# Score chunks copied out by ScalarE and folded in bf16 by VectorE, and merge transposes done by DMA, in an attention block with its gradients

## The chip, the cores and the metric

The kernel runs on one core of a Trainium2 chip. The core has five engines that run side by side, each with its own instruction queue worked off in order: TensorE (PE in the profile; PEld is its weight load), VectorE (DVE), ScalarE (ACT), GpSimd (POOL) and SyncE (SP), which here issues nearly all DMA transfers. Waits between engines go by semaphores. Data lies in SBUF (128 partitions); TensorE writes to PSUM, which VectorE and ScalarE read and GpSimd doesn't use here. The metric is the device time of one execution in microseconds; lower is better.

## The reference

A branchformer layer, forward and all gradients, for x and grad_out of shape [2, 4000, 144] in bf16. Cut to what matters:

```python
xa = layernorm(x)
q, k, v = split(xa @ w_qkv)
p = softmax(q @ k.T * 144 ** -0.5)             # 4000 x 4000 for each of the 2 batches
glob = (p @ v) @ w_att_out
u, g = split(gelu(xa @ w_mlp_in))
loc = (u * conv5(layernorm(g), dw_csgu)) @ w_mlp_out
m = concat(glob, loc)
out = x + (m + conv5(m, dw_merge)) @ w_merge
# and the vjp of out for grad_out: gradients of x and of the seven weights
```

`conv5` is a depthwise convolution with five taps along the sequence.

## The kernel before

A batch of 4000 positions is cut into 32 tiles of 125; both batches make 64 tiles, numbered through. A batch's position p * 32 + j lies on partition p in tile j, so that a shift along the sequence becomes a shift of the tile's number.

**The attention loop** (`phase_att`). Step s of its loop makes the scores of tile s and finishes earlier tiles. A tile's 4000 scores come in four chunks of 1000 (`c2` = 0 to 3). `products(q)` calls `quad`, which issues eight matmuls: scores of tile s, chunk q (two of 500 columns), and for tile s - 1, chunk q ^ 1, the product dP of the output gradient with the values (two of 500); each first over 128 rows of the contraction (L1304), then over the 16 left over (L1311). The results lie in two PSUM buffers `ps`, of which the pool `ps_sg` has exactly two.

- The scores' buffer is emptied by `S_min`: VectorE writes the negated scores in bf16 into `Pbuf` and their least into a column of `nm` in the same pass (L1326). After the fourth chunk a reduction over four columns gives the tile's least (L1328).
- `P_exp` turns a chunk of `Pbuf` into exponentials in place, on ScalarE, with that least as bias (L1332). All four chunks need the whole tile's least.
- dP's buffer is emptied by `PdP`: ScalarE copies it to `Sbuf` in bf16 (L1342), and VectorE multiplies it with `Pbuf` (L1344).
- `P_tr` (L1336) and `st_half` (L1518) transpose `Pbuf` and `Sbuf` into `PT` and `ST` by DMA, in halves of 16 blocks, for the products over keys: `Y_half` (L1353, with a reciprocal and small operations on three engines behind it) and `Z_half` (L1391).
- `X_group` (L1438) accumulates, over two tiles at a time, the gradient of the normalised input; VectorE adds it to `acc` in SBUF (L1444).

**The local branch** (`local_units`, L571 to L710) is cut into small units that are strewn over the attention loop's steps, for tiles 2 to 26 with batch 0 and again for tiles 34 to 60 with batch 1. Between the two, batch 1 is prepared (`prep_late`).

**The merge** (`Merge`, `tr_pieces`, `out_g`). After the attention, the forward output needs the transposes of attention output (h = 0) and local product (h = 1), 36 blocks each with the halo, for each batch: `transposes` does up to eight blocks with TensorE into one PSUM buffer (L1642), and ScalarE copies them to `YT[h]` (L1643), which for h = 0 is the storage of `goT` of batch 1. The 16 columns left over go the same way to `YS` (L1647, L1648). `out_g` multiplies from `YT` and `YS` (L1809, L1811). Both batches use the same `YT`, batch 0 first. Meanwhile `fill` issues matmuls for a weight gradient (`Hps`, L1724).

**The order.** A class `Planner` takes all instructions of the kernel and gives each engine a fixed order, by a list schedule with its own costs. Ready instructions are taken by their place in the program plus a lead from the table `LEAD`, whose keys name the stage (H, A, B, E, T), the engine, the tile and the size, and for some tiles the number of the instruction within a step.

Of the kernel before, what the change touches and what calls it, by code (L numbers as in the profile page):

```python
# [744 lines left out]
class Planner:  # L745
# [488 lines left out]
def phase_att(k, W, SS, A, head, E0, E1, prep, hooks):  # L1234
# [21 lines left out]
    PT = ab.tile([128, NB, 128], BF, name="PT")  # L1256
    ST = ab.tile([128, NB, 128], BF, name="ST")
    QBs = ab.tile([PB, NPB, 2, D], BF, name="QBs")
    qbr = [ab.tile([128, 512], BF, name="qb%d" % i) for i in range(3)]
    znr = [ab.tile([128, 256], BF, name="zn%d" % i) for i in range(2)]  # L1260

    def clr():
# [60 lines left out]
    def S_min(i, c2, src):  # L1323
        if c2 == 0:
            NM[i] = small.tile([PB, 5], F32, tag="nm", name="nm")
# [944 lines left out]
```

## Time and profile before

| | us |
|---|---|
| median of 3 runs | 1250.8 (1249.42 to 1252.87) |
| profiled execution | 1250.75 |
| its span, first to last instruction | 1249.0 |
| PE busy | 1182.0 (95%), 14424 matmuls |
| DVE busy | 1113.2 (89%), 3209 instructions |
| ACT busy | 867.3 (69%), 1590 |
| POOL busy | 348.1 (28%), 520 |

Granted TensorE clock: 0.998 of full speed. How to read the profile's lines: a group of instructions is given by line, engine, operation, names out<-in and shapes, then the count, the busy time in us and the mean ns of one, then the idle time of the engine just before them and what ended it. A row of a window has start:end, its length, then for each engine its busy time and the number of instructions, then the granted clock, the share of the DMA engines and GB/s. In a row of the timeline the two numbers in front are start and duration in us. In a row of one tile or line, three durations in ns are the least, the median and the largest. An operation's duration includes a part in which the next one has already begun, so in a full engine the distance of two starts is shorter. PE's busy time includes modelled ends; a busy PE is not PE at its peak.

### The profile page before, as it was taken

The numbers are of one execution on the slowest core, as the hardware profiler recorded it, in microseconds if no ns is written. First come the engines' busy times: TensorE is split into PE (matmuls) and PEld (weight loads), VectorE is DVE, ScalarE is ACT, GpSimd is POOL, SyncE is SP. The second block draws the span as 40 slices with busy tenths as digits, with TensorE's granted clock in tenths as the row PEclk, the third lists the DMA queues.
The fourth block names the chain that finished last, engine by engine and source line by source line (L and its number), as shares of the span: only waits on it lengthen the run. The fifth ranks groups of instructions, "written<-read, shape, count | busy, mean of one in ns | idle before, by whom it ended". The sixth has DMA issues, their size and how long they took to land.

```text
span 1249.0 us, 36648 instructions
## 1 busy us (share of the span) xinstructions
PE 1182.0 (95%) x14424; PEld 954.4 (76%) x14424; DVE 1113.2 (89%) x3209; ACT 867.3 (69%) x1590; POOL 348.1 (28%) x520
## 2 busy tenths in 40 slices
PE   6999999999999988999999999999999989999998
PEld 4677777777777767787777777777777767799997
DVE  8579999999999998987799999999999997779515
ACT  5897776777777666677877777777777756654741
POOL 7131323223232313301232332323232231033400
PEclk9999999999999999999999999999999999999999
DMA  4777787788787769998897877787968769967522
GB/s 137 148 151 152 138 181 141 159 170 153 161 160 143 157 132 189 177 162 190 170 170 140 167 154 151 162 162 144 183 138 168 149 132 197 208 173 182 148 56 57
DMA packets 662847, 193.94 MB, mean 155 GB/s; under 512 B 637619, under 2 KB 657093, under 8 KB 662653
## 3 DMA queue, kind: packets, MB, share of 16 engines
q1 hardware_dynamic: 661544, 190.20, 75.6%
q8 instruction: 113, 1.85, 0.6%
q0 software_dynamic: 592, 1.18, 0.3%
q14 instruction: 60, 0.49, 0.1%
q10 hardware_dynamic: 538, 0.21, 0.1%
HBM read 23.14 MB, written 16.69 MB: 32 GB/s over the span
## 4 chain that ended last, share of the span: by engine, by line
DVE 46%; PE 31%; ACT 10%; DMA 6%; issue 5%; POOL 1%; SPq 1%; DVEq 0%; ACTq 0%; POOLq 0%
DVE Pbuf L1326 12%; PE X L1438 7%; DVE Sbuf L1344 7%; DVE acc L1444 6%; PE ps L1304 5%; PE yz L1391 4%; DVE l_prod L637 3%; ACT Pbuf L1332 3%; PE yz L1353 3%; PE ps L1311 2%; PE po L1809 2%; ACT Sbuf L1342 2%; PE Hps L1724 2%; DMA PT<-Pbuf 2%; DMA ST<-Sbuf 1%
## 5 line engine op out<-in xcount | busy, mean ns | idle before, releaser
L1342 ACT CAST Sbuf<-ps 125x1000 bf16<-125x1000 f32 x252 | 251.8, 999 | 135.0 <-PE ps L1311 132.4
L1326 DVE TENSOR_SCALAR_CACHE_REDUCE Pbuf<-ps 125x1000 bf16<-125x1000 f32 x256 | 305.8, 1195 | 29.5 <-PE ps L1311 29.0
L1332 ACT ACTIVATE Pbuf<-Pbuf,nm 125x1000 bf16<-125x1000 bf16 x256 | 286.2, 1142 | 41.1 <-DVE nm L1328 41.1
L1438 PE MATMUL X<-QBs,Sbuf 125*125 125x144 bf16 x2048 | 296.4, 229 | 10.2 <-DVE acc L1444 5.5
L1438 PE MATMUL X<-QBs,Pbuf 125*125 125x144 bf16 x2048 | 291.7, 226 | 1.4 <-POOL QBs L1375 1.4
L1438 PEld LDWEIGHTS <-Sbuf 125*125 125x125 bf16 x2048 | 259.7, 137 | 30.4 <-issue 28.7
L1304 PE MATMUL ps<-xaT_m,qt 128*125 128x500 bf16 x1024 | 262.4, 375 | 14.7 <-DVE Pbuf L1326 8.7
L1438 PEld LDWEIGHTS <-Pbuf 125*125 125x125 bf16 x2048 | 260.7, 137 | 12.4 <-issue 12.0
L1444 DVE TENSOR_TENSOR acc<-X,acc 125x432 f32<-125x432 f32 (+1 forms) x373 | 200.1, 549 | 10.7 <-PE X L1438 9.2
L1344 DVE TENSOR_TENSOR Sbuf<-Sbuf,Pbuf 125x1024 bf16<-125x1024 bf16 x252 | 183.2, 729 | 3.2 <-ACT Sbuf L1342 2.5
L1304 PEld LDWEIGHTS <-qt 128*125 128x125 bf16 x1024 | 124.6, 137 | 60.2 <-issue 17.0
L1391 PE MATMUL yz<-xa_aug,ST 125*125 125x144 bf16 x2048 | 150.3, 228 | 12.4 <-ACT ty L1369 9.3
L1391 PEld LDWEIGHTS <-ST 125*125 125x125 bf16 x2048 | 140.1, 138 | 20.8 <-issue 14.8
L1353 PE MATMUL yz<-xa_aug,PT 125*125 125x145 bf16 x2048 | 148.6, 228 | 3.7 <-DMA PT<-Pbuf 2.6
L1353 PEld LDWEIGHTS <-PT 125*125 125x125 bf16 x2048 | 137.5, 137 | 14.0 <-issue 9.2
L1375 POOL TENSOR_TENSOR QBs<-g,g 125x144 bf16<-125x144 f32 x64 | 33.8, 528 | 285.7 <-ACT g L1374 271.9
L1311 PEld LDWEIGHTS <-qt 16*125 16x125 bf16 x1024 | 36.2, 128 | 98.9 <-issue 98.9
L1311 PE MATMUL ps<-XR,qt 16*125 16x500 bf16 x1016 | 110.9, 420 | 0.0
L637 DVE TENSOR_TENSOR l_prod<-ring,Wc 125x720 bf16<-125x720 bf16 x128 | 70.8, 576 | 0.0
L574 POOL TENSOR_SCALAR l_a<-l_sq 125x576 bf16<-125x576 bf16 x32 | 23.8, 743 | 165.7 <-ACT l_sq L572 157.4
L682 POOL TENSOR_TENSOR A_dwc<-l_fl,A_dwc 128x512 f32<-128x512 f32 (+2 forms) x48 | 39.8, 829 | 62.0 <-ACT l_fl L681 61.3
L665 POOL TENSOR_SCALAR l_w<-ring,nc,c 125x144 f32<-125x144 bf16 x60 | 34.8, 585 | 77.6 <-DVE nc L661 28.7
(545 smaller groups left out, 2067.4 us busy)
## 6 DMA issues: line engine op xcount, KB each, us to landing
Yn_d<-yn SPq DMA_DIRECT2D x64, 35.2 KB
Zn_d<-zn SPq DMA_DIRECT2D x64, 35.2 KB
ug_d<-ugr SPq DMA_DIRECT2D x32, 70.3 KB
PT<-Pbuf SPq DMA_TRANSPOSE x126
ST<-Sbuf SPq DMA_TRANSPOSE x126
go_h<-in_grad_out_dram SPq DMA_DIRECT2D x8, 252.0 KB
Yg<-Yn_d SPq DMA_DIRECT2D x8, 252.0 KB
Yg<-ug_d SPq DMA_DIRECT2D x8, 252.0 KB
```

Of the source, the lines that this page charges most:

```text
L637: nc.vector.tensor_tensor(prod[:, bi].rearrange("p a b -> p (a b)"), ring[:, a, p + bi:p + bi + 5, :].rearrange("p a b -> p (a b)"), W.Wc[ ...
L682: nc.gpsimd.tensor_tensor(acc, fl[r0:r1, 0:n], acc, op=ALU.add)
L1304: mm = nc.tensor.matmul(pp[r // 2][:, r % 2, 0:CH], QT[i][:, 2 * h, 0:PB], bs(i)[0].xaT_m[:, c * CH:(c + 1) * CH], start=True, stop=False)
L1311: nc.tensor.matmul(pp[r // 2][:, r % 2, 0:CH], QT[i][rs, 2 * h + 1, 0:PB], xr, start=False, stop=True)
L1326: nc.vector.tensor_scalar(pv(Pbuf, i % NPB, c2), src, -1.0, 3.0e38, op0=ALU.mult, op1=ALU.min, accum_out=NM[i][:, c2:c2 + 1])
L1332: nc.scalar.activation(v, v, ACT.Exp, bias=NM[i][:, 4:5], scale=-1.0)
L1342: nc.scalar.copy(pv(Sbuf, i % NDB, c2), src)
L1344: nc.vector.tensor_tensor(sc, sc, pchunk(i % NPB, c2), op=ALU.mult)
L1353: nc.tensor.matmul(Y, PT[0:PB, j, 0:PB], S.xa_aug[:, j, 0:D + 1], start=(j == 0), stop=(j == NB - 1))
L1391: nc.tensor.matmul(Z, ST[0:PB, j, 0:PB], S.xa_aug[:, j, 0:D], start=(j == 0), stop=(j == NB - 1))
L1438: nc.tensor.matmul(X[:, jj, :], l, r, start=(n_ == 0), stop=(n_ == len(ops) - 1))
L1444: nc.vector.tensor_tensor(av, X[:, 0:nj, :], av, op=ALU.add)
```

## The change

1. In `S_min`, chunks 0 and 2 (`SA`) no longer take VectorE's combined pass. ScalarE copies them from PSUM to `Pbuf`, negated. Once chunk 2 is there, VectorE takes the element-wise minimum of both chunks into a new tile `fold` (1000 wide), folds that onto itself twice (500, 250), and reduces the 250 left into the column of `nm` of chunk 2. Chunks 1 and 3 stay as they were. The last reduction now covers columns 1 to 3.
2. In the merge, batch 1's blocks for `YT` go through `turn`: GpSimd copies four blocks into one of three new tiles `ym` (partitions 125 to 127 of which stay zero), and a DMA transpose on SP's queue writes them to `YT`. That is 18 copies and 18 transposes. Batch 0 still uses TensorE. For this `YT` has blocks of 128 columns instead of 125, so `goT` of both batches grows by 108 columns.
3. The table `LEAD` is replaced by another, longer one: some 530 entries where there were some 170. It is cut out below.

```diff
     LEAD = {
-        "H ACT raw 144": -41, "H SP go_q 576": 145, "H DVE lnst 6": -4,
...
+        "H SP x_tp 1152": -167, "H DVE mhalf 32": -38, "H DVE wz 256": -50,
...
     }
...
     QBs = ab.tile([PB, NPB, 2, D], BF, name="QBs")
+    SA = (0, 2)
+    fold = ab.tile([PB, 2 * CH], BF, name="fold")
...
     def S_min(i, c2, src):
+        pb = i % NPB
         if c2 == 0:
             NM[i] = small.tile([PB, 5], F32, tag="nm", name="nm")
-        nc.vector.tensor_scalar(pv(Pbuf, i % NPB, c2), src, -1.0, 3.0e38, op0=ALU.mult, op1=ALU.min, accum_out=NM[i][:, c2:c2 + 1])
+        if c2 in SA:
+            nc.scalar.activation(pv(Pbuf, pb, c2), src, ACT.Copy, scale=-1.0)
+            if c2 == SA[-1]:
+                f = fold[:].rearrange("p (h a b) -> p h a b", h=2, b=PB)
+                nc.vector.tensor_tensor(f, pv(Pbuf, pb, SA[0]), pv(Pbuf, pb, SA[1]), op=ALU.min)
+                for w in (500, 250):
+                    nc.vector.tensor_tensor(fold[:, 0:w], fold[:, 0:w], fold[:, w:2 * w], op=ALU.min)
+                nc.vector.tensor_reduce(NM[i][:, c2:c2 + 1], fold[:, 0:250], axis=AX.X, op=ALU.min)
+        else:
+            nc.vector.tensor_scalar(pv(Pbuf, pb, c2), src, -1.0, 3.0e38, op0=ALU.mult, op1=ALU.min, accum_out=NM[i][:, c2:c2 + 1])
         if c2 == 3:
-            nc.vector.tensor_reduce(NM[i][:, 4:5], NM[i][:, 0:4], axis=AX.X, op=ALU.min)
+            nc.vector.tensor_reduce(NM[i][:, 4:5], NM[i][:, 1:4], axis=AX.X, op=ALU.min)
...
-        engs[0](dstm[:, j0 * PB:(j0 + n) * PB].rearrange("p (a b) -> p a b", b=PB), pm[:, 0:n, 0:PB])
+        engs[0](dstm[:, j0:j0 + n, 0:PB], pm[:, 0:n, 0:PB])
...
-        self.YT = [S1.goT, pm_.tile([128, NH * PB], BF, name="YT1")]
+        self.YT = [t[:].rearrange("p (a b) -> p a b", b=128) for t in (S1.goT, pm_.tile([128, NH * 128], BF, name="YT1"))]
+        self.ym, self.nym = [pm_.tile([128, 4, 128], BF, name="ym%d" % i) for i in range(3)], 0
+        for t in self.ym:
+            k.nc.gpsimd.memset(t[96:128], 0.0)
...
+    def turn(self, b, h, j0, n):
+        nc = self.k.nc
+        if n > 4:
+            self.turn(b, h, j0, 4)
+            return self.turn(b, h, j0 + 4, n - 4)
+        t = self.ym[self.nym % 3]
+        self.nym += 1
+        nc.gpsimd.tensor_copy(t[0:PB, 0:n, :], self.src[b][h][:, j0:j0 + n, 0:128])
+        nc.sync.dma_start_transpose(out=self.YT[h][:, j0:j0 + n, :], in_=t[:, 0:n, :].rearrange("p a b -> p (a b)"))
...
-                out.append(lambda h=h, j0=j0, n=n: transposes(k, W, self.src[b][h], None, self.YT[h], None, j0, n, (e, e)))
+                out.append(lambda h=h, j0=j0, n=n: self.turn(b, h, j0, n) if b else transposes(k, W, self.src[b][h], None, self.YT[h], None, j0, n, (e, e)))
...
-                        nc.tensor.matmul(po[:, q, :], YT[h][:, (i + kk) * PB:(i + kk + 1) * PB], VU[h][:, kk, :], start=(n_ == 0), stop=False)
+                        nc.tensor.matmul(po[:, q, :], YT[h][:, i + kk, 0:PB], VU[h][:, kk, :], start=(n_ == 0), stop=False)
...
-        S.goT = pa.tile([128, (NB + 4) * PB], BF, name="goT%d" % b)
+        S.goT = pa.tile([128, (NB + 4) * 128], BF, name="goT%d" % b)
```

115 rows, old and new, of the table LEAD are left out of this document.

## The prediction

> **What bounds the kernel now.** The execution falls into stages. I cut it at the moments when a tile's least score is finished and read, for each stage, the busy time of every engine.
>
> ```profile
> core 0: us, PE busy (x) PEld busy (x) DVE busy (x) ACT busy (x) POOL busy (x), PEclk, DMA share, GB/s
> 0.00:93.64 93.64, 80.93 (x827) 58.43 (x827) 69.14 (x199) 74.58 (x167) 40.67 (x77) 1.00 0.67 145
> 93.64:465.90 372.26, 352.03 (x4139) 277.69 (x4138) 369.40 (x1048) 268.32 (x485) 108.83 (x150) 1.00 0.79 154
> 465.90:634.35 168.45, 159.45 (x1930) 126.85 (x1929) 141.94 (x379) 123.00 (x210) 40.47 (x68) 1.00 0.92 177
> 634.35:1034.86 400.51, 384.86 (x4589) 305.00 (x4587) 398.87 (x1122) 289.45 (x522) 114.79 (x157) 1.00 0.79 156
> 1107.76:1249.00 141.24, 134.10 (x2036) 127.06 (x2034) 82.76 (x360) 69.78 (x142) 28.92 (x38) 1.00 0.47 123
> ```
>
> In the two long stretches in which a batch's local branch runs beside the attention (93.64 to 465.90 and 634.35 to 1034.86) VectorE is busy 369.40 + 398.87 = 768.3 of 772.8 us, 99.4%. ScalarE works 557.8 us there, 72%. In the other stages VectorE is not full. The chain of waits says the same: VectorE carries nearly half of it, TensorE a third.
>
> ```profile
> DVE 46%; PE 31%; ACT 10%; DMA 6%; issue 5%; POOL 1%; SPq 1%; DVEq 0%; ACTq 0%; POOLq 0%
> ```
>
> The pace per tile comes from the last reduction of the scores' least, one per tile, in windows over the two long stretches and over the stretch between them:
>
> ```profile
> L1328 DVE TENSOR_REDUCE nm<-nm x23: 118/148/158, 93.5 to 465.8; 125x1 f32<-125x4 f32 x23
> L1328 DVE TENSOR_REDUCE nm<-nm x25: 132/150/160, 634.2 to 1034.7; 125x1 f32<-125x4 f32 x25
> L1328 DVE TENSOR_REDUCE nm<-nm x5: 142/146/150, 523.8 to 584.5; 125x1 f32<-125x4 f32 x5
> ```
>
> That is 22 + 24 = 46 tiles in 372.3 + 400.5 us, 16.8 us each, where VectorE is full, and 4 tiles in 60.7 us, 15.2 us each, where it is not. In the middle of the latter TensorE never pauses:
>
> ```profile
> 530.00:565.00 35.00, 35.00 (x441) 28.20 (x440) 27.82 (x59) 25.34 (x42) 3.04 (x7) 1.00 0.97 161
> 600.00:635.00 35.00, 31.02 (x346) 23.48 (x344) 25.85 (x70) 31.69 (x63) 8.32 (x12) 1.00 0.87 181
> ```
>
> 35.00 / 441 = 79.4 ns per matmul. A tile of the long stretches has (4139 + 4589) / 46 = 190 matmuls, so TensorE alone would need about 15.1 us. That is an estimate, and the room for a VectorE saving: at most 1.7 us per tile, then TensorE takes over.
>
> **VectorE's part, per tile.** Removed: two of four passes over a chunk of scores. What an operation costs a full engine is the time from its start to the next start, shorter than its duration. Starts in us, then durations:
>
> ```profile
> 745.55 0.68 DVE L1344 TENSOR_TENSOR Sbuf<-Sbuf,Pbuf 125x1024 bf16<-125x1024 bf16 x1
> 746.15 0.36 DVE L1395 SCALAR_TENSOR_TENSOR zn<-yz,rl,ty 125x144 bf16<-125x144 f32 x1
> 746.43 0.44 DVE L638 TENSOR_TENSOR l_t<-l_prod 125x576 bf16<-125x576 bf16 x1
> 746.79 0.45 DVE L631 TENSOR_TENSOR l_sq<-l_z,l_a 125x576 bf16<-125x576 bf16 x1
> 747.16 1.19 DVE L1326 TENSOR_SCALAR_CACHE_REDUCE Pbuf<-ps 125x1000 bf16<-125x1000 f32 x1
> 748.28 0.08 DVE L1326 DVE_READ_ACCUMULATOR Pbuf<-ps 125x1 f32 x1
> 748.28 1.44 DVE L1344 TENSOR_TENSOR Sbuf<-Sbuf,Pbuf 125x1024 bf16<-125x1024 bf16 x1
> ...
> 750.53 0.29 DVE L639 TENSOR_TENSOR l_t<-l_t 125x288 bf16<-125x288 bf16 x1
> 750.74 1.19 DVE L1326 TENSOR_SCALAR_CACHE_REDUCE Pbuf<-ps 125x1000 bf16<-125x1000 f32 x1
> ...
> 752.46 0.15 DVE L1328 TENSOR_REDUCE nm<-nm 125x1 f32<-125x4 f32 x1
> 752.53 0.59 DVE L1444 TENSOR_TENSOR acc<-X,acc 125x432 f32<-125x432 f32 x1
> ```
> ```profile
> 1109.02 0.74 DVE L1821 TENSOR_REDUCE dx_s<-acc 125x4 f32<-125x576 f32 x1
> 1109.68 0.30 DVE L1824 SCALAR_TENSOR_TENSOR pj__20159<-acc,xa_aug 125x144 bf16<-125x144 f32 x1
> ```
>
> The pass takes 747.16 to 748.28, 1.12 us; the next instruction starts with its accumulator read, which therefore costs nothing. Removed: 2.24 us. Added: a fold of 1000, one of 500, one of 250, and a reduction of 250. Two-source bf16 operations take 0.60 (1024 elements), 0.36 (576) and 0.21 us (288); interpolated, 0.59 + 0.32 + 0.20. The reduction lies between 0.07 (4 elements) and 0.66 us (576 in f32); linearly 0.32. Sum 1.43, so 0.81 us saved on paper. The trace has no fold with a minimum; I take the rows of other two-source bf16 operations, since dtype, sizes and memory agree. The first fold also reads rows of 125 that don't touch, which no SBUF pair here does. If it streamed like the pass over PSUM (1.12), the saving would be 0.28; that is the low end.
>
> The passes removed are steady. What replaces them isn't:
>
> ```profile
> L1326 DVE TENSOR_SCALAR_CACHE_REDUCE Pbuf<-ps x256: 1161/1196/1212, 19.4 to 1078.2; 125x1000 bf16<-125x1000 f32 x128
> L1344 DVE TENSOR_TENSOR Sbuf<-Sbuf,Pbuf x252: 656/684/1772, 43.2 to 1087.6; 125x1024 bf16<-125x1024 bf16 x126
> L638 DVE TENSOR_TENSOR l_t<-l_prod x64: 419/451/1460, 96.6 to 1025.1; 125x576 bf16<-125x576 bf16 x64
> L1344 DVE TENSOR_TENSOR Sbuf<-Sbuf,Pbuf 125x1024 bf16<-125x1024 bf16 x252 | 183.2, 729 | 3.2 <-ACT Sbuf L1342 2.5 <-DMA zt<-zn 0.3
> L638 DVE TENSOR_TENSOR l_t<-l_prod 125x576 bf16<-125x576 bf16 x64 | 31.1, 486 | 0.1
> ```
>
> The scores' pass, read from PSUM, never exceeds 1212 ns. The two-source operations on SBUF reach 1772 and 1460; their means (729, 486) lie 73 and 67 ns above their least. Each fold will be held up likewise: 3 x 0.06 = 0.18 us per tile. That leaves 0.63.
>
> The Trainium skill has a rule that speaks against the change here ("SBUF — State Buffer", section "SBUF: two separate sides"): a VectorE operation with two SBUF inputs and a GpSimd operation that reads SBUF exclude each other for the whole instruction, and a VectorE operation reading PSUM is outside of it. The rows agree (spread up to 1772 against 1212). Were each fold to wait out half a GpSimd copy (0.76 us, the ring's, quoted below), three would cost 1.1 us, and 0.81 saved would turn into 0.3 lost, 15 us in 46 tiles; by the means above it costs the 0.18.
>
> A fold reads what the operation just before it wrote. In the changed program's order the four steps stand apart by one other VectorE instruction in most tiles, which covers the write-to-read delay; back to back they would stall. But the first fold waits for ScalarE's copy of the third chunk, and behind it in VectorE's queue stand the multiplications and accumulations that give TensorE its buffers back. I take 0.18 us per tile for such waits: VectorE now idles 4.5 us in 46 tiles, 0.1 each, and nearly three times that seems the price of hanging on a fuller ScalarE. So 0.45 us net x 46 tiles = **21 us**. Bounds: 0.81 x 46 = 37 us gained; at the low end (0.28 less 0.18 and 0.18) 4 us lost.
>
> **ScalarE's part.** Added: two copies of 125x1000 out of PSUM per tile. The copies of the other product are the same operation:
>
> ```profile
> 740.38 1.15 ACT L1332 ACTIVATE Pbuf<-Pbuf,nm 125x1000 bf16<-125x1000 bf16 x1
> 741.41 1.00 ACT L1342 CAST Sbuf<-ps 125x1000 bf16<-125x1000 f32 x1
> 742.28 0.43 ACT L1283 CAST qb<-pj 125x288 bf16<-125x288 f32 x1
> ```
> ```profile
> L1342 ACT CAST Sbuf<-ps 125x1000 bf16<-125x1000 f32 x252 | 251.8, 999 | 135.0 <-PE ps L1311 132.4
> ```
>
> A copy takes 742.28 - 741.41 = 0.87 us, so 1.74 per tile. Busy time was 557.8 / 46 = 12.1 us; it becomes 13.9 of about 16.35, 85%. The cover is ScalarE's idle time, most of it ahead of those very copies (132.4 us waiting for TensorE). Where the cover is thin it costs. Up to 93.64 ScalarE is busy 74.58 us, and five tiles bring 5 x 1.74 = 8.7: all hidden, or all paid. I take **3 us lost**. Between 600 and 635 us it is busy 31.69 of 35.00, and two tiles bring 3.5; **1 us lost**. The rest of that middle stage, and the last tiles, are TensorE's, so neither VectorE's gain nor ScalarE's load shows.
>
> **The merge's transposes.** In the second batch 72 TensorE transposes and 10 ScalarE copies go; 18 GpSimd copies of 512 elements and 18 DMA transposes on SP's queue come.
>
> ```profile
> 1195.24 0.60 PE L1647 MATMUL pm<-ident,Yr 125*80 125x125 bf16 x8
> 1195.68 0.60 PE L1642 MATMUL pm<-ident,Yg 125*128 125x125 bf16 x8
> L617 POOL COPY ring<-ring 125x576 bf16<-125x576 bf16 x8 | 6.1, 762 | 11.1 <-DVE ring L614 5.9 <-ACT ring L610 3.1 <-DVE rl L1359 2.0
> L1296 SPq DMA_TRANSPOSE qt<-qb x62: 1188/1210/2041, 45.5 to 1062.5; - x62
> ```
>
> Eight transposes take 0.44 us, so 72 are 4.0 us of TensorE, full for most of this stage (134.10 of 141.24). GpSimd gets at most 18 x 0.76 = 13.7 us, and is busy only 28.92 of the 141.24. SP holds each transpose of 512 elements for 1.21 us: 21.8 us, in a queue shared with loads of x, stores of results and the second batch's Zn, all of which wait behind a transpose that waits for its copy. Between 4 us gained and 4 lost (two late landings of about 2 us); I take **2 us gained**.
>
> The written-out leads of the planner all change too. That moves the order everywhere and can't be priced by a row; it is part of why the waits above are taken at 0.18 and not at nothing.
>
> **Sum.** -21 + 3 + 1 - 2 = -19. The profiled execution took 1250.75 us (span 1249.0), the median of the runs is 1250.8; so **1232 us**.
>
> **Rivals.**
> - TensorE is reached. ScalarE's cover holds and the folds cost their paper price: 0.81 x 46 = 37 us, less the head's 3 and plus the tail's 2, about 1215. For it: 16.0 us per tile stays above the 15.1 that TensorE needs. Against: between 523.8 and 584.5 TensorE's own pace was 15.2 with fewer matmuls, and three engines near full leave no slack.
> - ScalarE becomes the bound on PSUM, slower than before. Half of the quads now leave through ScalarE alone: 2 x 0.87 = 1.74 us, where VectorE and ScalarE drained them side by side in 1.12. If an exponential (741.41 - 740.38 = 1.03 us) stands in front as well, such a quad's buffers come back 1.65 us later. The gain's cover is 16.8 - 15.1 = 1.7 us per tile of TensorE slack; two quads late by more than 0.85 us each eat all of it. At 1.03 us each, 15.1 + 2.06 = 17.2 us per tile, 46 x 0.4 = 18 us lost, with the head 21: about 1270. For it: in the new order copies do stand behind exponentials. Against: between two quads TensorE has other matmuls to do, and ScalarE is not full.
> - The folds eat their gain. The first fold streams at the slow rate, or each is held up: 0.28 - 0.18 leaves 0.1 us, 5 us, which the head and the middle give back: 1250.
>
> **How the numbers follow.** My forecast (1222 to 1244) gets 0.42, TensorE reached 0.20, ScalarE the bound 0.27, folds eaten 0.11. About 0.3%, 3.7 us, is what a measurement can tell from no change. Faster: 0.42 + 0.20 + 0.02 of the last = 0.64; same 0.07; slower 0.29. The range runs from 1212, the paper price, to 1264, within the ScalarE case; what lies beyond is less than two in ten. As both signs carry weight, the likeliest case's own range stands beside it, 1222 to 1244.
>
> **What would show it.** Right: in the long stretches tiles 16.2 to 16.5 us apart; VectorE still above 96% busy, ScalarE near 85%; folds of about 0.65, 0.4 and 0.3 us in duration, with a tail where GpSimd holds them up; copies of the scores near 1.0 us. Wrong: a first fold near 1.1 us; VectorE idle before the first fold, waiting for ScalarE; TensorE waiting for buffers behind score copies; a head beyond 97 us for its five tiles; TensorE idle before the last outputs, waiting for a transpose to land.

## The result

The changed kernel took 1288.24 us (median of 4 runs, 1287.47 to 1289.65), the kernel before, timed beside it, 1251.84 us (1249.42 to 1253.3): a ratio of 1.030, interval 1.0284 to 1.0313. It is 36 us slower, where 19 us faster were forecast; the range ended at 1264.

The windows of the changed kernel are cut where the same tiles' least scores are finished as in the prediction's windows (head, long stretch, middle stage, long stretch); then come the last tiles and the merge, which begins when the last tile's least is finished:

```profile
0.00:103.48 103.48, 84.73 (x853) 60.40 (x854) 67.33 (x204) 84.22 (x179) 40.36 (x77) 1.00 0.58 135
103.48:480.49 377.01, 352.26 (x4146) 279.07 (x4146) 360.79 (x1053) 305.80 (x526) 113.32 (x150) 0.99 0.81 154
480.49:658.67 178.18, 163.00 (x1902) 129.75 (x1901) 130.59 (x366) 139.32 (x229) 41.23 (x68) 0.97 0.84 163
658.67:1071.49 412.82, 385.67 (x4544) 304.85 (x4542) 390.79 (x1119) 332.49 (x570) 114.60 (x157) 0.99 0.76 151
1071.49:1118.60 47.11, 45.62 (x541) 36.30 (x539) 32.74 (x78) 33.24 (x51) 6.13 (x12) 0.97 0.92 187
1118.60:1286.60 168.00, 159.23 (x2382) 151.63 (x2378) 101.02 (x394) 75.38 (x154) 50.97 (x78) 0.98 0.59 145
```

Of the 37.6 us that the span grew (1249.0 to 1286.6), the head has 9.8 (93.64 to 103.48), the middle stage 9.7 (168.45 to 178.18) and the two long stretches together 17.1 (772.8 to 789.8, 17.17 us a tile instead of 16.80). The last tiles took 1.8 us more (45.27 before), the merge 0.9 less (168.87 before). In the two long stretches VectorE did get less to do: 360.79 + 390.79 = 751.6 us busy instead of 768.3. But it now stands idle for 38 us there, where it idled 4.5 before. In the chain of waits VectorE had 46%; in the changed kernel no engine carries more than a third:

```profile
PE 33%; DVE 33%; ACT 17%; DMA 9%; issue 5%; SPq 2%; POOL 1%; ACTq 0%; DVEq 0%; POOLq 0%
```

ScalarE's share went from 10% to 17%. The groups of instructions say who waits for it; the first fence is the kernel before, the second the changed one, and the last column is the idle time of the engine ahead of the group, with what ended it:

```profile
L1391 PE MATMUL yz<-xa_aug,ST 125*125 125x144 bf16 x2048 | 150.3, 228 | 12.4 <-ACT ty L1369 9.3
L1444 DVE TENSOR_TENSOR acc<-X,acc 125x432 f32<-125x432 f32 (+1 forms) x373 | 200.1, 549 | 10.7 <-PE X L1438 9.2
```
```profile
L1389 ACT ACTIVATE Pbuf<-ps 125x1000 bf16<-125x1000 f32 x128 | 130.5, 1019 | 13.8 <-PE ps L1372 13.7
L1462 PE MATMUL yz<-xa_aug,ST 125*125 125x144 bf16 x2048 | 152.7, 231 | 32.4 <-ACT ty L1440 26.9
L1515 DVE TENSOR_TENSOR acc<-X,acc 125x432 f32<-125x432 f32 (+1 forms) x373 | 201.3, 548 | 34.1 <-PE X L1509 32.4
L1415 DVE TENSOR_TENSOR Sbuf<-Sbuf,Pbuf 125x1024 bf16<-125x1024 bf16 x252 | 175.0, 695 | 29.0 <-ACT Sbuf L1413 26.2 <-ACT Pbuf L1403 1.8
```

VectorE's multiplication waits 26.2 us for ScalarE's copy of the other product (2.5 before, by the prediction's row of L1344). TensorE waits 26.9 us for ScalarE's `ty` (9.3 before), and VectorE's accumulations 32.4 us for TensorE (9.2 before). So VectorE waits for ScalarE directly, and it waits more for TensorE, which itself waits more for ScalarE. These are sums over the whole run, though, and most of VectorE's lie outside the two long stretches, above all in the middle stage. In the stretches alone the two waits come to 12.3 us, and the rest of VectorE's 38 us there is made up of many small ones; the first two lines are the first stretch, the other two the second:

```profile
DVE acc L1515 <- PE X L1509: 4.8, 9, 1.1
DVE Sbuf L1415 <- ACT Sbuf L1413: 0.9, 3, 0.5
DVE Sbuf L1415 <- ACT Sbuf L1413: 3.5, 7, 1.2
DVE acc L1515 <- PE X L1509: 3.1, 5, 1.1
```

One place, from the timeline of all engines of the changed kernel (idle time ahead of an instruction and what ended it in brackets):

```profile
758.33 0.43 PE L1372 MATMUL ps<-XR,qt 16*125 16x500 bf16 x4
...
758.81 0.99 ACT L1413 CAST Sbuf<-ps 125x1000 bf16<-125x1000 f32 x1 [0.96 <-PE ps L1372]
...
759.70 1.01 ACT L1389 ACTIVATE Pbuf<-ps 125x1000 bf16<-125x1000 f32 x1
...
759.84 0.69 DVE L1415 TENSOR_TENSOR Sbuf<-Sbuf,Pbuf 125x1024 bf16<-125x1024 bf16 x1 [0.42 <-ACT Sbuf L1413]
...
760.74 0.68 DVE L1392 TENSOR_TENSOR fold<-Pbuf 125x1000 bf16<-125x1000 bf16 x1 [0.21 <-ACT Pbuf L1389]
...
761.25 1.01 PE L1365 MATMUL ps<-xaT_m,qt 128*125 128x500 bf16 x4
```

A quad is finished at 758.8. ScalarE copies its two halves one after the other, until 760.7; VectorE waits for the first and again for the second, and the next quad's scores begin at 761.25. TensorE did not stand still meanwhile; it had other matmuls. In the kernel before, VectorE took one of the two halves itself.

### The profile page after: what moved, and what is told of

It reads as the page before. It is cut to its first block, busy times and chain, and to the rows that moved or that the text cites. A ratio compares the mean times of both kernels' runs of the same rounds, so it can differ in the third digit from the quotient of the medians.

```text
span 1286.6 us, 36685 instructions
## 1 busy us (share of the span) xinstructions
PE 1190.5 (93%) x14352; PEld 962.0 (75%) x14352; DVE 1083.3 (84%) x3209; ACT 970.5 (75%) x1708; POOL 366.6 (28%) x541
## 4 chain that ended last, share of the span: by engine, by line
PE 33%; DVE 33%; ACT 17%; DMA 9%; issue 5%; SPq 2%; POOL 1%; ACTq 0%; DVEq 0%; POOLq 0%
PE X L1509 8%; DVE acc L1515 5%; DVE Pbuf L1397 5%; PE yz L1462 5%; PE ps L1365 5%; ACT Pbuf L1403 4%; DVE Sbuf L1415 4%; ACT Sbuf L1413 4%; PE yz L1424 3%; PE po L1893 3%; DMA PT<-Pbuf 2%; ACT Pbuf L1389 2%; DVE fold L1392 2%; DVE fold L1394 2%; PE Hps L1795 2%
## 5 line engine op out<-in xcount | busy, mean ns | idle before, releaser
L1403 ACT ACTIVATE Pbuf<-Pbuf,nm 125x1000 bf16<-125x1000 bf16 x256 | 289.7, 1144 | 38.6 <-DVE nm L1399 38.1
L1365 PE MATMUL ps<-xaT_m,qt 128*125 128x500 bf16 x1024 | 266.9, 376 | 21.2 <-ACT Sbuf L1413 10.0
L1509 PEld LDWEIGHTS <-Sbuf 125*125 125x125 bf16 x2048 | 261.8, 138 | 23.1 <-issue 22.7
L1515 DVE TENSOR_TENSOR acc<-X,acc 125x432 f32<-125x432 f32 (+1 forms) x373 | 201.3, 548 | 34.1 <-PE X L1509 32.4
L1415 DVE TENSOR_TENSOR Sbuf<-Sbuf,Pbuf 125x1024 bf16<-125x1024 bf16 x252 | 175.0, 695 | 29.0 <-ACT Sbuf L1413 26.2
L1462 PE MATMUL yz<-xa_aug,ST 125*125 125x144 bf16 x2048 | 152.7, 231 | 32.4 <-ACT ty L1440 26.9
L1462 PEld LDWEIGHTS <-ST 125*125 125x125 bf16 x2048 | 143.9, 140 | 44.4 <-issue 37.9
L1397 DVE TENSOR_SCALAR_CACHE_REDUCE Pbuf<-ps 125x1000 bf16<-125x1000 f32 x128 | 152.9, 1194 | 18.1 <-PE ps L1372 17.8
L1424 PE MATMUL yz<-xa_aug,PT 125*125 125x145 bf16 x2048 | 153.7, 231 | 8.0 <-DMA PT<-Pbuf 5.9
L1424 PEld LDWEIGHTS <-PT 125*125 125x125 bf16 x2048 | 141.4, 139 | 20.6 <-issue 10.8
L1389 ACT ACTIVATE Pbuf<-ps 125x1000 bf16<-125x1000 f32 x128 | 130.5, 1019 | 13.8 <-PE ps L1372 13.7
L1446 POOL TENSOR_TENSOR QBs<-g,g 125x144 bf16<-125x144 f32 x64 | 35.5, 554 | 274.4 <-ACT g L1445 259.9
L637 DVE TENSOR_TENSOR l_prod<-ring,Wc 125x720 bf16<-125x720 bf16 x128 | 65.4, 539 | 2.3 <-ACT ring L610 2.2
```

Source lines behind the costliest of these rows:

```text
L637: nc.vector.tensor_tensor(prod[:, bi].rearrange("p a b -> p (a b)"), ring[:, a, p + bi:p + bi + 5, :].rearrange("p a b -> p (a b)"), W.Wc[ ...
L1365: mm = nc.tensor.matmul(pp[r // 2][:, r % 2, 0:CH], QT[i][:, 2 * h, 0:PB], bs(i)[0].xaT_m[:, c * CH:(c + 1) * CH], start=True, stop=False)
L1389: nc.scalar.activation(pv(Pbuf, pb, c2), src, ACT.Copy, scale=-1.0)
L1397: nc.vector.tensor_scalar(pv(Pbuf, pb, c2), src, -1.0, 3.0e38, op0=ALU.mult, op1=ALU.min, accum_out=NM[i][:, c2:c2 + 1])
L1403: nc.scalar.activation(v, v, ACT.Exp, bias=NM[i][:, 4:5], scale=-1.0)
L1415: nc.vector.tensor_tensor(sc, sc, pchunk(i % NPB, c2), op=ALU.mult)
```

## The experiments

### The parts of the change

e1_lead is the kernel before with the changed kernel's table of leads and nothing else.

```diff
     LEAD = {
-        "H ACT raw 144": -41, "H SP go_q 576": 145, "H DVE lnst 6": -4, "H DVE lndm 8": -171, "H POOL rstd_x 8": 130, "H PE hps 0": 41,
...
+        "H SP x_tp 1152": -167, "H DVE mhalf 32": -38, "H DVE wz 256": -50, "H DVE raw 1008": -86, "H POOL two 1008": -45, "H POOL M1T 144": 70,
...
```

> The kernel before with the changed kernel's table of leads, nothing else. Theory 'ScalarE' (the added copies make ScalarE late, and TensorE waits for buffers): the table is not the cause, so the time stays near 1251, within 1240 to 1265. Rival 'order' (the new table gives a poor order): 1275 or more, most of the 37 us. Some keys number ScalarE's and VectorE's writes within a step otherwise in this kernel, so a loss is an upper bound of what the table costs.

Measured: 1278.51 us, ratio 1.021 (1.0176 to 1.0244), as the rival 'order' had it. e2_fold is the other half: copies, folds and reduction as in the changed kernel, but the old table, with the score groups' keys named by chunk so that each lead keeps its meaning.

```diff
+        if c2 in SA:
+            nc.scalar.activation(pv(Pbuf, pb, c2), src, ACT.Copy, scale=-1.0)
+            if c2 == SA[-1]:
...
+                nc.vector.tensor_tensor(f, pv(Pbuf, pb, SA[0]), pv(Pbuf, pb, SA[1]), op=ALU.min)
...
+                    c = "%s DVE Pbuf 1000 %d" % (c[0], chunk)
```

> The folds and ScalarE's score copies alone, merge as before, with the table of leads of before; the keys' numbering is changed so that each lead still meets the same operation (by chunk), which alone leaves the order of before untouched. Theory 'ScalarE': slower, 1275 to 1295, with TensorE waiting for the one yz buffer and the two ps buffers behind ScalarE. Rival 'order': the table is to blame, so with the old one the forecast gain shows, 1225 to 1245.

Measured: 1310.56 us, ratio 1.0462 (1.0423 to 1.0501), beyond both ranges. A table made for the one program costs the other some 22 to 26 us, so neither run alone prices the copies and folds. The fair pair is n0 (before) and n1_fold (copies, folds and reduction), both with an empty table.

```diff
-    LEAD = {
...
-    }
+    LEAD = {}
```

> The kernel before with an empty table of leads (plain program order as priority). No theory says how much; 1270 to 1330. It is the base for the next one.

> The folds and ScalarE's score copies in the kernel before, with an empty table of leads. Theory 'ScalarE': slower than the empty table without folds by 10 to 40 us. Rival 'order' (the part itself is good, the leads are not): faster than it by 10 to 25 us.

Measured: 1268.3 and 1303.82 us (two runs of each). Without any lead the copies and folds cost 35.5 us; with each kernel's own table the whole change costs 36.4. The table is worth 15 to 17 us to either kernel. So the loss doesn't come from the table alone.

e3_turn has only the merge's transposes as DMA transposes.

```diff
-                out.append(lambda h=h, j0=j0, n=n: transposes(k, W, self.src[b][h], None, self.YT[h], None, j0, n, (e, e)))
+                out.append(lambda h=h, j0=j0, n=n: self.turn(b, h, j0, n) if b else transposes(k, W, self.src[b][h], None, self.YT[h], None, j0, n, (e, e)))
```

> The merge's transposes by DMA alone, attention and table of leads as before. Both theories: a small gain, 1246 to 1251 (4.0 us of TensorE saved, at most 4 us lost to late landings). 1255 or more would say that the transposes by DMA cost something the changed kernel's last stage hides.

Measured: 1251.26 us, ratio 0.9987 (0.9969 to 1.0005): no difference that can be told. e4_nofold is the changed kernel without folds and without the reduction over them; the least is taken over chunks 1 and 3 alone.

```diff
-            if c2 == SA[-1]:
...
-                nc.vector.tensor_reduce(NM[i][:, c2:c2 + 1], fold[:, 0:250], axis=AX.X, op=ALU.min)
...
-            nc.vector.tensor_reduce(NM[i][:, 4:5], NM[i][:, 1:4], axis=AX.X, op=ALU.min)
+            nc.vector.tensor_reduce(NM[i][:, 4:5], NM[i][:, 1:4:2], axis=AX.X, op=ALU.min)
```

> The changed kernel without the folds and their reduction: the tile's least is taken over chunks 1 and 3 alone, so that VectorE loses 1.6 us of work per tile while ScalarE keeps its copies. Rival 'folds' (their time on VectorE eats the gain): 1288 falls by 46 x 1.0 us or more, to 1240 or below. Theory 'ScalarE': VectorE isn't what sets the pace, so at most 10 us are won, 1278 to 1290.

Measured: 1273.12 us, ratio 1.0173 (1.0142 to 1.0205). Even with the folds free, and VectorE's busy time down to 15.0 us a tile, the kernel is 21 us slower than before. The folds' cost cannot be what turned the gain into a loss. The folds are not free either: without them the two long stretches took 770.9 us, 19 less than in the changed kernel and 2 less than before, so that this run loses its time in the head (104.41 us) and the middle stage (180.02). Its order was planned anew.

### VectorE's time and ScalarE's, each by itself

e5_relief takes from VectorE what the prediction hoped to take, and adds nothing: from tile 4 on the passes over chunks 0 and 2 take 750 of their 1000 columns. e6_actload adds to the kernel before two ScalarE copies a tile of 800 columns, from SBUF to a tile that nobody reads.

```diff
+        n = 3 if i >= NPB and c2 in (0, 2) else 4
-        nc.vector.tensor_scalar(pv(Pbuf, i % NPB, c2), src, -1.0, 3.0e38, op0=ALU.mult, op1=ALU.min, accum_out=NM[i][:, c2:c2 + 1])
+        nc.vector.tensor_scalar(pv(Pbuf, i % NPB, c2)[:, :, 0:n], src[:, :, 0:n], -1.0, 3.0e38, op0=ALU.mult, op1=ALU.min, accum_out=NM[i][:, c2:c2 + 1])
```
```diff
+        if c2 in (0, 2):
+            nc.scalar.copy(scr[:], bs(i)[0].xaT_m[0:PB, 0:800])
```

> The kernel before, with VectorE's pass over chunks 0 and 2 cut to 750 of 1000 columns from tile 4 on (the rest of those chunks keeps an older tile's values, so results are wrong by that). ScalarE gets nothing. VectorE loses 2 x 0.26 = 0.52 us per tile. Theory 'VectorE bounds the long stretches and the copies on ScalarE spoilt it': 46 x 0.5 = 24 us faster, 1222 to 1235. Rival 'TensorE's own pace is reached at once' (the long stretches can't go below about 16.5 us per tile whatever VectorE does): 1240 to 1252.

> The kernel before, with two more ScalarE copies per tile (800 columns SBUF to SBUF into a tile that nobody reads, about 0.87 us each), placed where the score copies would be; VectorE, TensorE and PSUM as before. Theory 'ScalarE's load alone delays what TensorE and VectorE wait for': 1265 to 1290. Rival 'it is the PSUM buffers that leave through ScalarE, not its load': within 5 us of 1252.

Measured: e5_relief 1244.72 us, ratio 0.995 (0.9934 to 0.9966); e6_actload 1283.65 us, ratio 1.0264 (1.0208 to 1.032). The relief of VectorE brings 7 us, the load on ScalarE costs 32, and that without a buffer of PSUM held or an instruction of VectorE changed. Three variations: e8_actone has one of the two copies (chunk 2), e9_actlow both with a lead of 350, which puts them behind more urgent work, and e7_actrelief takes time away from ScalarE (exponentials of chunks 0 and 2 over half their columns, from tile 4 on).

```diff
-        if c2 in (0, 2):
+        if c2 == 2:
```
```diff
+        "H ACT scr 800": 350, "A ACT scr 800": 350, "B ACT scr 800": 350, "E ACT scr 800": 350,
```
```diff
-        v = pv(Pbuf, i % NPB, c2)
+        v = pv(Pbuf, i % NPB, c2)[:, :, 0:2 if i >= NPB and c2 in (0, 2) else 4]
```

> As the kernel with two extra ScalarE copies per tile, with one (at chunk 2). Theory 'load counts by the microsecond': half of the 32 us, 1262 to 1272. Rival 'a threshold': under 6 us, below 1258.

> As the kernel with two extra ScalarE copies per tile, with a lead of 350 for these copies, so that the planner takes them only where it sees nothing else ready on ScalarE. Theory 'load': the order helps little, 1272 to 1290. Rival 'placement' (the copies stand in front of work that TensorE waits for): the loss goes, below 1262.

> The kernel before, with the exponentials of chunks 0 and 2 taken on half of the columns from tile 4 on (the other half keeps negated scores, so results are wrong by that): ScalarE loses 2 x 0.42 us per tile, nothing else changes. Theory 'ScalarE's load counts although it idles' (it stands on the path through TensorE and VectorE at every tile): 8 to 20 us faster, 1232 to 1244. Rival 'only above about 80% does ScalarE matter': within 4 us of 1252.

Measured: e8_actone 1274.12 us (1.0165, 1.0133 to 1.0197), e9_actlow 1268.08 us (1.0101, 1.0055 to 1.0148), e7_actrelief 1258.5 us (1.005, 1.0033 to 1.0067). Putting the copies behind other work thus takes away about half of e6_actload's loss, less than the rival 'placement' had and more than the theory. The last is the awkward one: less work on ScalarE, and slower, which neither side expected. The planner makes a new order for every changed program, and the old leads no longer fit it. v1_pool, an attempt at a better version (one of ScalarE's small products, `g1`, made by GpSimd), was slower too: 1257.32 us, ratio 1.0043 (1.0027 to 1.0059).

```diff
-        nc.scalar.activation(g1[:], qb[:, 1, 0:D], ACT.Copy, scale=rl[:])
+        nc.gpsimd.tensor_scalar(g1[:], qb[:, 1, 0:D], rl[:], 1.0, op0=ALU.mult, op1=ALU.mult)
```

> The kernel before, with g1 (125x144, once per tile) made by GpSimd and not by ScalarE: 0.3 us per tile less on ScalarE, about 0.5 more on GpSimd. Theory 'load counts': 3 to 6 us faster, less what GpSimd's reads hold VectorE up, 1245 to 1252. Rival 'idle ScalarE time is free': 1251 to 1256.

So all of these mix a load with a new order.

### The same, with every order held

In the next runs the planner is told the old sizes (or, for added copies, a cost of nothing), so that each engine's instructions stand in exactly the order of the kernel named; only work differs. f1_dve, f2_actless and f3_actmore are the kernel before with the edits of e5, e7 and e6.

```diff
+        if aps_o and aps_o[0].bass_ap.tensor.name.startswith("Pbuf") and e == "DVE" and n == 750:
+            n = 1000
```
```diff
+        if aps_o and aps_o[0].bass_ap.tensor.name.startswith("scr"):
+            return 0.0, 0.0
```

> Before's kernel with the order of every engine kept exactly (the planner is told the old size); from tile 4 on the VectorE passes over chunks 0 and 2 take three of four blocks of each half (750 of 1000 columns), so the result is not the reference's there. That takes about 0.52 us a tile from VectorE and nothing from the others. If VectorE sets the pace of the score stretches, the time falls by 0.52 x 46 = 24 us, to about 1228. If TensorE's own pace is reached soon after, it falls by 5 to 10 us (1242 to 1247), as it did with a re-planned order.

> Before's kernel, order of every engine kept exactly; ScalarE's exponentials of chunks 0 and 2 run over half their columns from tile 4 on (the result is not the reference's). Some 0.9 us a tile less on ScalarE. If ScalarE's time is already on the path in the kernel before (its work decides when PSUM and the merge come free), the time falls by 5 to 15 us. If its idle time covers what it does, nothing moves: 1249 to 1255.

> Before's kernel with the order of all its instructions kept exactly, and two more ScalarE copies a tile (800 columns, from SBUF to a tile that nobody reads) for which the planner is told a cost of nothing. Theory of ScalarE's load (the copies' 1.7 us a tile are not covered): 1265 to 1285, as with the re-planned order (1284). Theory of the order (a re-planned order is what costs): within 5 us of before, 1247 to 1257.

Measured: f1_dve 1242.46 us (0.9918, 0.9894 to 0.9943); f2_actless 1251.68 us (0.9995, 0.9984 to 1.0007); f3_actmore 1275.02 us (1.0183, 1.0151 to 1.0214). Their windows over the two long stretches, f1_dve first, then f3_actmore:

```profile
93.89:460.29 366.40, 348.88 (x4139) 276.02 (x4138) 359.82 (x1049) 268.34 (x485) 107.88 (x150) 1.00 0.80 157
...
629.67:1028.18 398.51, 384.43 (x4591) 304.91 (x4590) 388.82 (x1123) 290.70 (x522) 114.66 (x157) 1.00 0.81 157
```
```profile
106.11:484.84 378.73, 351.87 (x4121) 276.84 (x4119) 368.93 (x1048) 299.63 (x529) 108.66 (x150) 1.00 0.76 152
...
654.75:1063.99 409.24, 389.50 (x4590) 307.05 (x4591) 399.84 (x1123) 324.77 (x570) 115.42 (x157) 1.00 0.79 153
```

In f1_dve VectorE's busy time falls by 768.27 - 748.64 = 19.6 us and the stretches by 772.8 - 764.9 = 7.9: four tenths of the relief arrive. In f3_actmore ScalarE's rises by 624.4 - 557.8 = 66.6 us and the stretches grow by 15.2: nearly a quarter of the load arrives, with VectorE's work (768.8 us) and every order unchanged. VectorE's idle time there grows from 4.5 to 19.2 us, which is nearly the whole of it. What VectorE waits for is in the waits of f3_actmore, over the whole run and then, for the second line, in each of the two stretches:

```profile
DVE Pbuf L1334 <- PE ps L1319: 35.6, 37, 3.3
DVE Sbuf L1354 <- ACT Sbuf L1352: 14.5, 27, 1.3
...
DVE Sbuf L1354 <- ACT Sbuf L1352: 6.5, 11, 1.3
...
DVE Sbuf L1354 <- ACT Sbuf L1352: 4.3, 9, 0.8
```

The first two were 29.0 and 2.5 us in the kernel before, and the wait for ScalarE's copy in the stretches was 0.3: of the 14.7 us by which VectorE's idle time grew there, 10.5 are this wait. The profiled run of f3_actmore is the slowest of its four, with a span 28.4 us above the kernel before; 12.5 of them are in the head, at a lower clock (last section). f2_actless takes time off ScalarE (two of a tile's four exponentials run over half their columns; 523.4 us busy in the stretches instead of 557.8), and nothing moves. So added time on ScalarE cost and saved time brought nothing; but the two runs touch different operations in different places, so they don't show where between them the cost begins.

f4_after_act, f6_after_actq and f5_after_dve hold the order of the changed kernel. From tile 4 on the first two cut the added ScalarE copies to a half (`n = 2`, shown) and a quarter (`n = 1`) of their columns, the third VectorE's two remaining passes to 750 columns.

```diff
-            nc.scalar.activation(pv(Pbuf, pb, c2), src, ACT.Copy, scale=-1.0)
+            n = 2 if i >= NPB else 4
+            nc.scalar.activation(pv(Pbuf, pb, c2)[:, :, 0:n], src[:, :, 0:n], ACT.Copy, scale=-1.0)
```

> The changed kernel with its order on every engine kept exactly; from tile 4 on ScalarE's copies of chunks 0 and 2 out of PSUM run over half the columns (the result is not the reference's). That takes some 0.8 us a tile from ScalarE. Theory of ScalarE's load: 15 to 25 us less than the changed kernel, 1263 to 1273. Theory of the order: within 5 us of 1288. VectorE the bound: within 5 us of 1288 as well.

> The changed kernel with its order on every engine kept exactly; from tile 4 on VectorE's two remaining passes out of PSUM (chunks 1 and 3) run over three of four blocks of each half (750 of 1000 columns), so the result is not the reference's. That takes some 0.5 us a tile from VectorE. If VectorE still sets the pace: 20 to 24 us less than the changed kernel, 1264 to 1268. If ScalarE and TensorE set it now: at most 8 us less, 1280 to 1290. In between, both take turns, as in the kernel before (10 us less for the same relief).

> The changed kernel with its order kept exactly; ScalarE's copies of chunks 0 and 2 run over a quarter of the columns from tile 4 on (the result is not the reference's). Half the columns gave 1274 us. If ScalarE's time is what costs, a quarter gives another 5 to 8 us: 1265 to 1270. If the rest is the order and the places of the instructions, the time stays at 1271 to 1276. Either way what is left above 1245 to 1250 is not the copies' time.

Measured: f4_after_act 1274.25 us (1.018, 1.0157 to 1.0203), f6_after_actq 1273.98 us (1.0171, 1.014 to 1.0202), f5_after_dve 1276.0 us (1.0186, 1.0154 to 1.0219). The first halving of the copies gives 14 us back, the second nothing. Relief of VectorE gives 12. So in the changed kernel both engines' time counts. But with the copies down to a quarter 20 us of the loss remain, although ScalarE, with 587.0 us in the stretches, is only 29 above the kernel before. The waits named above remain too: VectorE 23.1 us for the copy of the other product, TensorE 27.2 for `ty`, VectorE 35.4 for X. They are not made by the length of the copies. And this head is among the 20 us:

```profile
0.00:102.32 102.32, 84.13 (x852) 59.99 (x852) 67.45 (x204) 82.92 (x179) 40.87 (x77) 1.00 0.58 137
```

The head keeps its full copies for the first four tiles in that run, and keeps 8.7 us of the loss.

## Why the prediction was wrong

**The cover was not there.** The step that failed is "The cover is ScalarE's idle time": 1.74 us of added copies a tile were priced at nothing in the 46 tiles. With every order held, added copies of 1.45 us a tile cost 15.2 us there (f3_actmore), and halving the change's own copies gave 14 us back (f4_after_act). The copies' own price held: 1019 ns in the mean (the row of L1389), where the other product's copy took 999, and ScalarE came to 638.3 / 46 = 13.9 us a tile, as forecast. What did not hold is that an engine idle for a quarter of its time can take the work for free. Its 132.4 us of waiting for TensorE were not a reserve to be spent: ScalarE runs its queue in order, and a copy that fits into the idle time on average still makes the one behind it late. In f3_actmore the 132.4 us fell to 93.3, and VectorE waited for the late copies of the other product, without PSUM, folds or a new order: +23 us in all by the medians.

**The head.** Of 8.7 us of added copies in the first five tiles the prediction took 3 as paid ("all hidden, or all paid"). All were paid, and a little more: 9.8. With an empty table the copies and folds cost the head nearly as much (96.66 us in n0, 105.91 in n1_fold). The average that the prediction looked at, 74.58 of 93.64 us, hid where ScalarE has no idle time. A finer window of the kernel before:

```profile
70.00:90.00 20.00, 18.57 (x215) 14.56 (x215) 14.82 (x38) 20.00 (x41) 7.90 (x10) 1.00 0.87 165
```

20.00 of 20.00. The runs with dummy copies agree. e8_actone, with half as many, and e9_actlow, whose copies give way to other work:

```profile
0.00:99.67 99.67, 82.91 (x851) 59.97 (x852) 72.08 (x204) 80.08 (x177) 40.99 (x78) 1.00 0.63 140
```
```profile
0.00:93.74 93.74, 80.07 (x815) 57.60 (x816) 67.73 (x190) 82.43 (x177) 38.42 (x75) 1.00 0.65 143
```

ScalarE has 5.5 us more in the one and the head is 6.0 longer. In the other it has 7.9 more and the head is as before: the copies went where ScalarE had idle time. But in this run, the slowest of its four, the stretches took 797.0 us, 24 more than before. Moving the work does not make it free either.

**VectorE's saving was smaller in effect, not in price.** The folds cost what the prediction interpolated. From the changed kernel's VectorE timeline:

```profile
742.27 0.68 DVE L1392 TENSOR_TENSOR fold<-Pbuf 125x1000 bf16<-125x1000 bf16 x1
742.87 0.30 DVE L1515 TENSOR_TENSOR acc<-X,acc 125x144 f32<-125x144 f32 x1
743.09 0.41 DVE L1394 TENSOR_TENSOR fold<-fold 125x500 bf16<-125x500 bf16 x1
743.41 0.60 DVE L1515 TENSOR_TENSOR acc<-X,acc 125x432 f32<-125x432 f32 x1
743.93 0.28 DVE L1394 TENSOR_TENSOR fold<-fold 125x250 bf16<-125x250 bf16 x1
744.12 1.20 DVE L1397 TENSOR_SCALAR_CACHE_REDUCE Pbuf<-ps 125x1000 bf16<-125x1000 f32 x1
...
745.24 0.41 DVE L1395 TENSOR_REDUCE nm<-fold 125x1 f32<-125x250 bf16 x1
745.57 0.68 DVE L1415 TENSOR_TENSOR Sbuf<-Sbuf,Pbuf 125x1024 bf16<-125x1024 bf16 x1
```

Start to start 0.60, 0.32, 0.19 and 0.33 us, against 0.59, 0.32, 0.20 and 0.32. The low end, a first fold at 1.12, did not come about. Yet VectorE's busy time fell by 16.7 us in the stretches where 0.63 x 46 = 29 were forecast. Most of the difference seems to lie in how its instructions follow each other. Without a standstill the next one starts some 80 ns before the end of the one in front, and each standstill loses this overlap. Counted in the traces, VectorE stood still ahead of 38 instructions in the stretches before and of 211 in the changed kernel: 173 x 0.08 = 14 us, an estimate. f1_dve agrees: its shorter passes (932 ns in the mean instead of 1194) take 92 x 0.262 = 24.1 us off, and with 58 more standstills 19.6 were seen. In 96 of these cases (15 before) the wait is some 34 ns, for what the instruction just in front wrote; the new order put steps of the local branch directly behind each other:

```profile
766.51 0.46 DVE L638 TENSOR_TENSOR l_t<-l_prod 125x576 bf16<-125x576 bf16 x1
767.00 0.31 DVE L639 TENSOR_TENSOR l_t<-l_t 125x288 bf16<-125x288 bf16 x1
767.34 0.31 DVE L643 TENSOR_TENSOR l_gc<-l_t,l_prod 125x288 bf16<-125x288 bf16 x1
```

The prediction had looked at this only for the folds, which do stand apart in most tiles. And the prediction let each us of VectorE count in full. By f1_dve it counts 0.4: 99.4% busy in the stretches was a sign of a full engine, not of the only bound. (The Trainium skill, "Perfetto Trace Analysis", section "Identifying the Most-Contended Engine", takes the engine with the highest occupancy for the one to optimize first. Here relieving it did help, by 10 us in f1_dve, but by less than half of what was taken off it.)

**The waits.** The prediction added 0.18 us a tile for VectorE hanging on ScalarE. Its idle time in the stretches grew from 0.1 to 38.2 / 46 = 0.83 us a tile. Of its signs of being wrong three came true: "VectorE idle before the first fold", "TensorE waiting for buffers behind score copies" and "a head beyond 97 us". The first two were minor: 8.1 us in all ahead of the fold, against 26.2 ahead of the multiplication, and 2.4 us for TensorE behind score copies. Of its signs of being right, the durations of folds and copies came true; VectorE came to 95% busy in the stretches, ScalarE to 81%.

**The middle stage** was priced at 1 us and lost 9.7. f3_actmore, with the order held, lost only 1.5 there, e1_lead, with the leads alone, 6.2, f6_after_actq, with quarter copies, 7.5. So most of it is not the copies' time. In the last two and in the changed kernel the granted clock of this stage was 0.96 to 0.97.

**The transposes** were forecast at 2 us gained between 4 and -4; e3_turn shows 0.8 us, not distinguishable from nothing. Where TensorE's saved 4 us went stays open; in the changed kernel the merge took 168.0 us instead of 168.87, at a clock of 0.98.

**The rival.** The slower case, "ScalarE becomes the bound on PSUM", gave 17.2 us a tile and 18 us lost in the stretches; 17.17 and 17.1 were measured. That they agree so closely is luck, for its mechanism is half of the truth at most. The quad above leaves PSUM through ScalarE alone, as it said, and TensorE's waits for the two buffers behind ScalarE rose from 1.9 to 12.4 us in the whole run; but dummy copies that touch no PSUM cost nearly as much. It also took the head at 3 us and the middle stage at no more than 1, and so ended at 1270.

**What stays open.** f3_actmore's copies are 800 columns; scaled by ScalarE's busy time in the stretches (80.5 us added by the change, 66.6 by f3) its 23 us become some 28. VectorE's relief of 16.7 us at 0.4 gives 7 back. That leaves about 15 of the 36 us, a rough estimate: by stages it leaves some 5 us in the stretches and 8 in the middle stage. f6_after_actq, from the other side, leaves 20 with the head and what its quarter copies still cost among them. This rest lies, as far as the runs tell, in the new order or in the new waits (a tile's least now hangs on two ScalarE copies); the runs don't separate the two, since no run had the new waits in the old order. One hint: VectorE's long waits for X and TensorE's for `ty` are there with either table and with none (31.2 and 31.6 us in e2_fold, 46.6 and 31.2 in n1_fold), and absent without the copies out of PSUM (14.7 and 8.1 in e1_lead, 12.6 and 12.0 in n0). No version that does the whole computation was faster than the kernel before; e3_turn can't be told from it.

## What to carry to other kernels

Idle time of an engine that runs its queue in order is not free cover: here a quarter of the load placed into it came back as time, because others waited for what stood behind. Before such time is spent, add the bare load (a copy that nobody reads) with the order held, and see what it costs; taking load off elsewhere on the same engine told another number here. And an average over a stage hides its full minutes: read the busy time in windows as short as the work that is to be hidden, and test a full engine's share by shortening its work before counting each of its microseconds as gain.

## What the runs showed of the hardware

In some of the stages that got longer the granted clock was lower. In the middle stage the changed kernel had 0.97 where the kernel before had 1.00, and TensorE needed 163.00 us / 1902 = 85.7 ns a matmul instead of 159.45 / 1930 = 82.6; for a like mix of matmuls that is 1902 x 3.1 ns = 5.9 us of TensorE's time in that stage. The head of f3_actmore had 0.92:

```profile
0.00:106.11 106.11, 87.90 (x827) 61.74 (x828) 69.51 (x199) 84.47 (x179) 40.83 (x77) 0.92 0.55 128
```

There TensorE took 87.90 us for the 827 matmuls for which the kernel before took 80.93, so that part of this run's 12.5 us in the head goes with the clock. The means hide steps: the trace has the clock at full speed but for stretches of 3.41 us, or a multiple of that, at half; in this head one of 13.65 us, from 24.69 on. One of three in the changed kernel's middle stage, with the 3.41 us ahead of it:

```profile
579.25:582.66 3.41, 1.62 (x16) 0.80 (x13) 1.57 (x3) 3.41 (x6) 0.49 (x1) 1.00 0.62 136
582.66:586.07 3.41, 3.41 (x28) 3.41 (x29) 0.69 (x1) 0.86 (x4) 0.00 (x0) 0.50 0.91 203
```

TensorE was busy 1.62 of the 3.41 us ahead; ahead of the other two it was 1.32 and 1.74. The Trainium skill ("TensorE: Matmul & The Clock Gate", section "Part 1: The HAM clock gate (the "warmup" mystery)") says that the clock is gated by how busy TensorE has lately been. These rows fit it; a wait of TensorE would then cost twice. But f6_after_actq's and e8_actone's heads, slower than before too, kept 1.00, and whether the clock is a cause of the longer stages or goes with them wasn't tried.

The folds were held up now and then, as the other two-source operations on SBUF, but rarely: the longest first fold took 1582 ns, with a least of 666, a median of 678 and a mean of 715, 49 above the least. For this fold the prediction's 60 ns was about right; a wait of half a GpSimd copy for each, by which it drew the rule of the shared port to 15 us lost, did not come.

```profile
L1392 DVE TENSOR_TENSOR fold<-Pbuf x64: 666/678/1582, 26.8 to 1113.2; 125x1000 bf16<-125x1000 bf16 x64
L1392 DVE TENSOR_TENSOR fold<-Pbuf 125x1000 bf16<-125x1000 bf16 x64 | 45.8, 715 | 8.5 <-ACT Pbuf L1389 8.1
```
